# Holding the identity in the TensorE array across the sums of a decode attention kernel

## Chip, cores, metric

The kernel runs on one core of a Trainium2 chip. The metric is the device time of one execution in microseconds (us), taken as the median of repeated runs; "span" is the length of one profiled execution.

TensorE is written PE, and its weight loads PEld, since the profile records them apart. DVE is VectorE, ACT is ScalarE, SP issues the large transfers. A "chunk" is 32768 tokens of one head. There are 64 chunks (32 heads, 2 for each), and each has a K and a V load of 8.39 MB.

## The reference

One decode step of gated attention and a small feed-forward block, cut to what matters:

```python
def _A_ref(x, k_cache, v_cache, wq, wo):          # H, Sk, Dh = 32, 65536, 128
    q = ((x @ wq).reshape(B, Sq, H, Dh)).transpose(0, 2, 1, 3)
    scores = jnp.einsum("bhqd,bhkd->bhqk", q, k_cache) * (Dh ** -0.5)
    p = _softmax(scores, axis=-1)
    o = jnp.einsum("bhqk,bhkd->bhqd", p, v_cache)
    return o.transpose(0, 2, 1, 3).reshape(B, Sq, H * Dh) @ wo
# a = _A_ref(...); b = swiglu(x); return g * a + (1 - g) * b
```

The two caches are 1.07 GB in bf16 and are read once. Everything else is small.

## The kernel before

Tokens lie on partitions, so a score is a sum over the free axis. DVE multiplies K by q in place. PE then does most of the sum: with the identity as weights, sixteen matmuls of 512 columns accumulate sixteen slices of 8 head elements into 512 columns of a PSUM tile, and DVE reduces the last factor of 8.

```python
def group(key, parts, reads, writes):
    def fn():
        for out_ap, pairs in parts:
            for i, (a, b) in enumerate(pairs):
                ins = nc.tensor.matmul(              # a weight load and a matmul
                    out_ap, lhsT=a, rhs=b, start=(i == 0), stop=(i == len(pairs) - 1)
                )
        return ins
    op("PE", key, fn, reads, writes)

def block(n, j, m):                                  # m = 128 of a chunk's 256 columns of tokens
    dve("products", lambda: nc.vector.tensor_tensor(out=w, in0=w, in1=q_rep, op=ALU.mult), ...)
    B = 512 // R                                     # R = 8
    group(("sums", s, j, m, r),
          [(S_ps[r][:, b : b + B, :],
            [(ident, w[:, b : b + B, i * R : (i + 1) * R]) for i in range(Dh // R)])
           for b in range(0, m, B)],
          names + ["ident"], [("S_ps", r)])
# ... cut: gather (the last factor of 8, on DVE), exponential on ACT
# pv(n): 64 matmuls, weights are 4 columns of probabilities, 512 columns of V move
```

A chunk has two blocks of 32 sums and one value product of 64 matmuls. Three SBUF slots of 8.39 MB turn: while one is worked on, loads for the other two are issued. PE's instructions for the middle heads are a loop; the other engines' are written out.

```python
for n in range(N - 1):
    if n:
        load("k", n, [KPP])      # each waits until the last reader of its slot is done
        load("v", n, [KPP])
    for j in range(0, KPP, m):
        block(n, j, m)
        # ... cut: gather, exponential
    pv(n)
```

The softmax here doesn't subtract the row's maximum and nothing guards it: scores larger than these inputs give would overflow.

## Time and profile before

| | before |
|---|---|
| time, median of 3 | 2522.19 us |
| span of the profiled run | 2518.0 us |
| DMA rate, 100 to 2400 us | 434 GB/s |
| weight loads | 9115, of which 4096 of the identity for sums |

The first fence holds lines of the profile page: busy time, share of the span and number of instructions of each engine; busy tenths in 40 equal slices (9 is 90% or more), with the granted PE clock and the DMA rate; DMA queues with packets, MB and share of the 16 engines' span; the chain that ended last, by engine.

```profile
PE 1975.5 (78%) x9115; PEld 821.6 (33%) x9115; DVE 1268.3 (50%) x290; ACT 98.0 (4%) x402; POOL 1.9 (0%) x9
...
PE   4787877877778778778787787787877877878788
PEld 2233332333323333333333333333333332333334
...
DMA  9999999999999999999999999999999999999998
GB/s 423 431 432 432 434 434 437 433 433 433 433 436 434 435 433 436 434 433 433 434 435 436 433 433 433 434 434 434 435 434 436 433 433 433 433 435 436 435 433 369
...
q1 hardware_dynamic: 20880, 1087.78, 99.8%
q8 instruction: 16, 0.26, 0.0%
...
DMA 46%; PE 39%; DVE 13%; ACT 1%; another core or an unknown queue 0%; issue 0%; SPq 0%; DVEq 0%
```

DMA is full from the first slice to the last but one (9 tenths or more in each, the main queue at 99.8%). PE looks busy as well, at 78%, and the chain gives it 39%. Neither makes PE the limit. 78% leaves 22% of the span free (overlapping records are counted once in it: 704 sums of S_ps_102 of 382 ns each, 269 us, are 157.7 us on the page). And the chain runs through an instruction that frees a slot even if the load it lets go then waits behind other loads: at 1013.70 us it passes from 13.99 us of a value product to a K load of 34.86 us. The list of issues shows that queue (operation and count; the last column is the median us from issue to landing):

```profile
slot_67<-in_A_v_cache_dram SPq DMA_DIRECT2D x21, 32.7
...
slot_67<-in_A_k_cache_dram SPq DMA_DIRECT2D x21, 36.0
```

A load needs 19.3 us at 434 GB/s (8.39 MB over the rate), so by this estimate 13 to 17 us of older transfer are still ahead of it when it is issued.

The timeline of one chunk (start in us, length in us, engine, line, operation, output and inputs, count, then in brackets the idle time before it and what ended it):

```profile
1057.33 8.69 PE L265 MATMUL S_ps_101<-slot_67,ident 128*128 128x512 bf16 x32 [6.79 <-DVE slot_67 L324]
...
1066.99 7.08 PE L265 MATMUL S_ps_102<-slot_67,ident 128*128 128x512 bf16 x32
```

```profile
1057.73 0.15 PEld L265 LDWEIGHTS S_ps_101<-slot_67,ident 128*128 128x128 bf16 x1 [0.28 <-issue]
...
1066.98 6.59 PEld L265 LDWEIGHTS S_ps_102<-slot_67,ident 128*128 128x128 bf16 x32
```

The first block of a chunk comes after idle time and begins at half clock: the trace's clock records grant 0.5 of full speed from 1053.8 to 1060.6 us, and in the same view its weight loads start at 1057.73, 1058.16 and 1058.58, some 0.43 us apart. The second block runs at full clock (1.00 granted from 1066.98 to 1074.06); such matmuls are called warm here.

The last line concerns the end of the kernel, where the last value products run:

```profile
2511.11 1.74 PE L251 MATMUL m_c<-P_sb_84,slot_65 128*128 128x1 bf16 x60 [1.23 <-issue]
```

"issue" is idle time for which the profile finds no wait.

### The profile page before, as it was taken

How to read it: one execution, taken by the hardware profiler on the slowest of the kernel's cores; microseconds unless marked ns; L12 is line 12 of the kernel's file. 1: busy time of each engine (PE TensorE's matmuls, PEld its weight loads, DVE VectorE, ACT ScalarE, POOL GpSimd, SP SyncE). 2: the span in 40 equal slices, each digit the busy share in tenths (PEclk: the TensorE clock that was granted, in tenths of full speed). 3: DMA queues.
4: the chain of work that ended last, by engine and by line, in shares of the span. 5: the costliest groups of instructions: out<-in, count | busy, mean ns of one | idle time of the engine just before them, and what ended most of it. 6: DMA issues, size and time to landing. Idle time of an engine off the chain costs nothing.

```text
span 2518.0 us, 19423 instructions
## 1 busy us (share of the span) xinstructions
PE 1975.5 (78%) x9115; PEld 821.6 (33%) x9115; DVE 1268.3 (50%) x290; ACT 98.0 (4%) x402; POOL 1.9 (0%) x9
## 2 busy tenths in 40 slices
PE   4787877877778778778787787787877877878788
PEld 2233332333323333333333333333333332333334
DVE  3455364464553554645535546445455464464554
ACT  0000000000000000000000000000000000000000
POOL 0000000000000000000000000000000000000000
PEclk8888989989889889898898899898988989989898
DMA  9999999999999999999999999999999999999998
GB/s 423 431 432 432 434 434 437 433 433 433 433 436 434 435 433 436 434 433 433 434 435 436 433 433 433 434 434 434 435 434 436 433 433 433 433 435 436 435 433 369
DMA packets 20906, 1088.09 MB, mean 432 GB/s; under 512 B 2450, under 2 KB 2580, under 8 KB 2836
## 3 DMA queue, kind: packets, MB, share of 16 engines
q1 hardware_dynamic: 20880, 1087.78, 99.8%
q8 instruction: 16, 0.26, 0.0%
q14 instruction: 6, 0.05, 0.0%
q10 hardware_dynamic: 4, 0.00, 0.0%
HBM read 1087.77 MB, written 0.00 MB: 432 GB/s over the span
## 4 chain that ended last, share of the span: by engine, by line
DMA 46%; PE 39%; DVE 13%; ACT 1%; another core or an unknown queue 0%; issue 0%; SPq 0%; DVEq 0%
PE O_ps L251 18%; DMA slot_67<-in_A_k_cache_dram 16%; DMA slot_66<-in_A_k_cache_dram 15%; DMA slot_65<-in_A_k_cache_dram 14%; PE S_ps_101 L265 11%; PE S_ps_102 L265 9%; DVE slot_67 L324 4%; DVE slot_66 L324 4%; DVE slot_65 L324 3%; DVE S_sb_82 L349 2%; PE m_c L251 1%; DMA slot_65<-in_A_v_cache_dram 1%; ACT P_sb_83 L274 1%; PE m_x L265 0%
## 5 line engine op out<-in xcount | busy, mean ns | idle before, releaser
L265 PE MATMUL S_ps_101<-slot_65,ident 128*128 128x512 bf16 x672 | 196.5, 465 | 133.8 <-DVE slot_65 L324 133.8
L265 PE MATMUL S_ps_101<-slot_66,ident 128*128 128x512 bf16 x672 | 193.5, 459 | 133.5 <-DVE slot_66 L324 133.5
L265 PE MATMUL S_ps_101<-slot_67,ident 128*128 128x512 bf16 x704 | 195.2, 446 | 125.0 <-DVE slot_67 L324 125.0
L324 DVE TENSOR_TENSOR slot_67<-slot_67,q_bc_79 128x16384 bf16<-128x16384 bf16 (+1 forms) x28 | 208.2, 7469 | 144.0 <-DMA slot_67<-in_A_k_cache_dram 144.0
L349 DVE TENSOR_REDUCE S_sb_82<-S_ps_102 128x128 f32<-128x1024 f32 (+1 forms) x67 | 78.8, 1176 | 391.5 <-PE S_ps_102 L265 391.5
L324 DVE TENSOR_TENSOR slot_65<-slot_65,q_bc_78 128x16384 bf16<-128x16384 bf16 x22 | 190.2, 8688 | 148.1 <-DMA slot_65<-in_A_k_cache_dram 148.1
L324 DVE TENSOR_TENSOR slot_66<-slot_66,q_bc_78 128x16384 bf16<-128x16384 bf16 (+1 forms) x24 | 190.6, 7977 | 136.5 <-DMA slot_66<-in_A_k_cache_dram 120.9
L324 DVE TENSOR_TENSOR slot_66<-slot_66,q_bc_79 128x16384 bf16<-128x16384 bf16 x20 | 172.9, 8688 | 123.9 <-DMA slot_66<-in_A_k_cache_dram 123.9
L324 DVE TENSOR_TENSOR slot_65<-slot_65,q_bc_79 128x16384 bf16<-128x16384 bf16 x20 | 172.9, 8688 | 118.5 <-DMA slot_65<-in_A_k_cache_dram 118.5
L324 DVE TENSOR_TENSOR slot_67<-slot_67,q_bc_78 128x16384 bf16<-128x16384 bf16 x20 | 172.9, 8688 | 117.5 <-DMA slot_67<-in_A_k_cache_dram 117.5
L251 PE MATMUL O_ps<-slot_67,P_sb_83 128*4 128x512 bf16 x704 | 156.4, 383 | 28.8 <-ACT P_sb_83 L274 18.3
L251 PE MATMUL O_ps<-slot_65,P_sb_83 128*4 128x512 bf16 x704 | 153.7, 379 | 19.6 <-ACT P_sb_83 L274 19.6
L251 PE MATMUL O_ps<-slot_66,P_sb_84 128*4 128x512 bf16 x704 | 153.7, 379 | 19.3 <-ACT P_sb_84 L274 19.3
L265 PE MATMUL S_ps_102<-slot_67,ident 128*128 128x512 bf16 x704 | 157.7, 382 | 3.1 <-DVE slot_67 L324 3.0
L265 PEld LDWEIGHTS S_ps_101<-slot_65,ident 128*128 128x128 bf16 x672 | 75.9, 116 | 254.6 <-DVE slot_65 L324 144.4
L265 PEld LDWEIGHTS S_ps_101<-slot_66,ident 128*128 128x128 bf16 x672 | 75.0, 115 | 252.0 <-DVE slot_66 L324 144.3
L265 PEld LDWEIGHTS S_ps_101<-slot_67,ident 128*128 128x128 bf16 x704 | 76.8, 112 | 243.1 <-DVE slot_67 L324 136.1
L251 PE MATMUL O_ps<-slot_67,P_sb_84 128*4 128x512 bf16 x640 | 139.7, 379 | 18.3 <-ACT P_sb_84 L274 18.3
L251 PE MATMUL O_ps<-slot_65,P_sb_84 128*4 128x512 bf16 x640 | 139.7, 379 | 18.3 <-ACT P_sb_84 L274 18.3
L251 PE MATMUL O_ps<-slot_66,P_sb_83 128*4 128x512 bf16 x640 | 139.7, 379 | 17.5 <-ACT P_sb_83 L274 17.5
L265 PE MATMUL S_ps_102<-slot_66,ident 128*128 128x512 bf16 x672 | 148.8, 379 | 2.1 <-DVE slot_66 L324 2.1
L265 PE MATMUL S_ps_102<-slot_65,ident 128*128 128x512 bf16 x672 | 148.6, 379 | 0.2 <-DVE slot_65 L324 0.2
(83 smaller groups left out, 860.6 us busy)
## 6 DMA issues: line engine op xcount, KB each, us to landing
slot_66<-in_A_k_cache_dram SPq DMA_DIRECT2D x4, 2048.0 KB, 24.6
slot_67<-in_A_k_cache_dram SPq DMA_DIRECT2D x4, 2048.0 KB, 30.6
slot_65<-in_A_wq_dram SPq DMA_DIRECT2D x1, 4096.0 KB, 12.2
slot_66<-in_A_wo_dram SPq DMA_DIRECT2D x1, 4096.0 KB, 31.3
slot_65<-in_A_v_cache_dram SPq DMA_DIRECT2D x1, 4096.0 KB, 23.2
slot_65<-in_A_v_cache_dram SPq DMA_DIRECT2D x1, 2048.0 KB, 27.7
slot_65<-in_B_w_gate_dram SPq DMA_DIRECT2D x1, 1792.0 KB, 34.9
slot_65<-in_B_w_up_dram SPq DMA_DIRECT2D x1, 1792.0 KB, 38.6
```

Of the source, the lines that this page charges most:

```text
L251: ins = nc.tensor.matmul(out_ap, lhsT=a, rhs=b, start=start and i == 0, stop=stop and i == len(pairs) - 1,)
L265: ins = nc.tensor.matmul(out_ap, lhsT=a, rhs=b, start=(i == 0), stop=(i == len(pairs) - 1))
L274: "ACT", key, lambda: nc.scalar.activation(out=out_ap, in_=in_ap, func=func, **kw),
L324: "products", lambda: nc.vector.tensor_tensor(out=w, in0=w, in1=q_rep, op=ALU.mult),
L349: lambda: nc.vector.tensor_reduce(out=S_sb[b][:, :m], in_=S_ps[r][:, :m, :], axis=AXIS.X, op=ALU.add),
```

## The change

The identity is to be loaded into the array once for each block; the other 31 matmuls use the weights that the array holds. The intent is to spare 3962 of the 4096 identity loads.

```diff
         def fn():
+            held = None
             for out_ap, pairs in parts:
                 for i, (a, b) in enumerate(pairs):
-                    ins = nc.tensor.matmul(
-                        out_ap, lhsT=a, rhs=b, start=(i == 0), stop=(i == len(pairs) - 1)
-                    )
+                    first, last = i == 0, i == len(pairs) - 1
+                    if a is held:
+                        ins = nc.tensor.add_instruction(
+                            mybir.InstMatmult(
+                                name=nc.get_next_instruction_name(), engine=mybir.EngineType.PE,
+                                ins=[nc.tensor.lower_ap(b), weights],
+                                outs=[nc.tensor.lower_ap(out_ap)],
+                                start_tensor_calc=first, stop_tensor_calc=last,
+                                tile_size=(P, P), tile_position=(0, 0), ldweights=False,
+                            )
+                        )
+                    else:
+                        ins = nc.tensor.matmul(out_ap, lhsT=a, rhs=b, start=first, stop=last)
+                        weights = ins.ins.ins[1]
+                    held = a
             return ins
```

## The prediction

> **What bounds the kernel now.** DMA. The slice table has the DMA row at 9 in all slices but the last; the queue table gives the main queue 99.8% of the 16 engines' span. The stretch table gives 434 GB/s in every stretch of 400 to 500 us between 100 and 2400 us; 1087.78 MB at that rate is 2506 us of a span of 2518. [...]
>
> The chain of waits reads DMA 46%, PE 39%, DVE 13%. The 39% is no gain to be had: the chain walks from a load back to what freed its slot, but loads queue behind each other. A K load (8.39 MB) takes 19.3 us at 434 GB/s, and the issue list gives 36 us to landing (V: 32.5): some 17 and 13 us of older transfer are queued at issue. A slot freed earlier only lengthens that queue.
>
> Per 38.6 us of transfer (one K, one V load) PE needs, by the timeline, 8.4 to 10 and 7.07 us for two blocks of sums and 13.97 for the value product: about 30 us.
>
> **What changes.** In 134 blocks (4096 matmuls) the identity is loaded once each: 3962 weight loads of 98 to 116 ns go, about 425 us of PEld's 821.6. Nothing is added or moved; the other engines keep their order. But a load already overlaps the matmul before it: 32 warm matmuls take 7.07 us, 221 ns each; value products, with four-column weights, 218. [...] Cold matmuls at the head of first blocks start every 427 ns with 0.28 us between loads; they gain nothing. In all 8 to 17 us of PE time, which no DMA waits for.
>
> **Critical path.** Head: weights, K0 and V0 are queued within 5 us, before any sums. Middle: DMA bound. Tail: the last sums end before 2504.3 and their exponentials by 2505.4, while value pieces land up to about 2510; then unchanged products, a scale and the output DMA. The PE stall of 1.23 us at 2509.88, which the timeline calls "issue", may be instruction supply; with fewer PE instructions it may shift or vanish, worth up to about 1 us.
>
> **Prediction.** 2521.5 us, 8 in 10 between 2518.0 and 2525.0. Faster by over 2%: 0.01; within: 0.97; slower: 0.02.
>
> **What would show it.** Weight loads 9115 down to 5153; PEld busy near 395 us. Warm blocks of sums 6.9 to 7.05 us; first blocks still 8 to 10 us, 427 ns matmuls at their head. 434 GB/s unchanged; K issue to landing longer by at most 0.5 us. DVE's waits for K loads unchanged in total within 10 us.
>
> **What would make it wrong.** [...] both sum blocks at 427 ns are 27 us, with 14 for the value product 41 us against 38.6, and PE would become the limit. If each matmul without its own load waited for the pipe (379 ns, its shown duration), sums would take 24 us, 38 in all: just short of binding. [...] short stretches (404 to 448 GB/s) show no order by PE activity.

No trace or run shows: a ceiling for the DMA rate, of which the trace has only the measured 434 GB/s; the terms of the saving in PE time; and the mechanisms behind two dangers, that the array stays at half clock for want of weight loads, and that weight loads hinder DMA (the 27 and 41 us are for the first of the two). The saving came to 8 to 17 us of PE time in all. It was the author's estimate, 2 to 5 ns for each warm matmul, and the 6.9 to 7.05 us for a warm block follow from it. The forecast of 2521.5 us does not rest on these terms, since no DMA waits for that PE time.

## The result

| | before | after |
|---|---|---|
| median, same rounds | 2521.9 us (4 runs) | 2521.67 us (4 runs) |
| ratio, 95% interval | | 0.9997 (0.998 to 1.0014) |
| weight loads | 9115 | 5153 |
| PEld busy | 821.6 us | 410.4 us |
| PE busy | 1975.5 us | 1980.9 us |

Ratios are the mean time of one kernel's fast runs over that of the other's of the same rounds, so not quite the ratio of the medians quoted.

The page of the profile after, the same lines as before:

```profile
PE 1980.9 (79%) x9115; PEld 410.4 (16%) x5153; DVE 1268.7 (50%) x290; ACT 97.9 (4%) x402; POOL 1.9 (0%) x9
...
PEld 1111111111111111111111111111111111111113
...
DMA  9999999999999999999999999999999999999998
GB/s 423 431 432 433 434 435 435 433 435 437 433 434 433 434 433 435 436 436 433 434 435 435 433 434 433 434 434 437 434 436 433 434 437 433 434 433 433 433 431 361
...
q1 hardware_dynamic: 20880, 1087.78, 99.7%
q8 instruction: 13, 0.21, 0.0%
...
DMA 44%; PE 41%; DVE 13%; ACT 1%; issue 0%; another core or an unknown queue 0%; SPq 0%; DVEq 0%; ACTq 0%
```

Half of the weight load time is gone, and little else moved. The list of issues after shows the same queue ahead of each load:

```profile
slot_67<-in_A_v_cache_dram SPq DMA_DIRECT2D x21, 32.6
...
slot_67<-in_A_k_cache_dram SPq DMA_DIRECT2D x21, 36.0
```

The timeline of one chunk after, where a block now has one matmul with a load (L279) and 31 without (L269):

```profile
1017.42 0.61 PE L279 MATMUL S_ps_101<-slot_65,ident 128*128 128x512 bf16 x1 [4.88 <-DVE slot_65 L338]
1017.82 8.94 PE L269 MATMUL S_ps_101<-slot_65,ident 128*128 128x512 bf16 x31
...
1026.59 0.38 PE L279 MATMUL S_ps_102<-slot_65,ident 128*128 128x512 bf16 x1
1026.81 6.85 PE L269 MATMUL S_ps_102<-slot_65,ident 128*128 128x512 bf16 x31
```

The warm block runs from 1026.59 to 1026.81 + 6.85 = 1033.66: 7.07 us, as before. Start to start it is (6.85 - 0.379) / 30 = 216 ns. A count over all recorded sums gives the same median, 216 ns, before and after. So not even PE became faster. And the pause near the end is still there:

```profile
2512.66 2.01 PE L251 MATMUL m_c<-P_sb_84,slot_65 128*128 128x1 bf16 x70 [1.22 <-issue]
```

The time is unchanged, then. Two reasons are possible, and each alone would be enough. Either PE gained something that a full DMA hid (theory A), or PE gained nothing because the loads already ran behind the matmuls (theory B). The runs below separate them.

### The profile page after: what moved, and what is told of

It is laid out like the page before. It is cut to its first block, busy times and chain, and to the rows that moved or that the text cites. A ratio compares the mean times of both kernels' runs of the same rounds, so it can differ in the third digit from the quotient of the medians.

```text
span 2519.9 us, 15461 instructions
## 1 busy us (share of the span) xinstructions
PE 1980.9 (79%) x9115; PEld 410.4 (16%) x5153; DVE 1268.7 (50%) x290; ACT 97.9 (4%) x402; POOL 1.9 (0%) x9
## 2 busy tenths in 40 slices
DMA packets 20903, 1088.04 MB, mean 432 GB/s; under 512 B 2450, under 2 KB 2580, under 8 KB 2836
## 4 chain that ended last, share of the span: by engine, by line
DMA 44%; PE 41%; DVE 13%; ACT 1%; issue 0%; another core or an unknown queue 0%; SPq 0%; DVEq 0%; ACTq 0%
PE O_ps L251 18%; DMA slot_67<-in_A_k_cache_dram 16%; DMA slot_65<-in_A_k_cache_dram 14%; DMA slot_66<-in_A_k_cache_dram 14%; PE S_ps_101 L269 11%; PE S_ps_102 L269 9%; DVE slot_67 L338 4%; DVE slot_66 L338 4%; DVE slot_65 L338 3%; DVE S_sb_82 L363 2%; PE m_c L251 1%; PE S_ps_101 L279 1%; PE m_x L279 1%; ACT P_sb_83 L288 1%; DMA slot_65<-in_A_wq_dram 0%; PE S_ps_102 L279 0%
## 5 line engine op out<-in xcount | busy, mean ns | idle before, releaser
L269 PE MATMUL S_ps_101<-slot_67,ident 128*128 128x512 bf16 x680 | 191.3, 450 | 0.0
L269 PE MATMUL S_ps_101<-slot_65,ident 128*128 128x512 bf16 x651 | 187.1, 458 | 0.0
L269 PE MATMUL S_ps_101<-slot_66,ident 128*128 128x512 bf16 x650 | 185.3, 455 | 0.0
L269 PE MATMUL S_ps_102<-slot_67,ident 128*128 128x512 bf16 x680 | 152.4, 382 | 0.0
L269 PE MATMUL S_ps_102<-slot_65,ident 128*128 128x512 bf16 x651 | 143.9, 379 | 0.0
L269 PE MATMUL S_ps_102<-slot_66,ident 128*128 128x512 bf16 x650 | 143.9, 379 | 0.0
L279 PE MATMUL S_ps_101<-slot_65,ident 128*128 128x512 bf16 x21 | 12.8, 608 | 134.5 <-DVE slot_65 L338 134.5
L279 PE MATMUL S_ps_101<-slot_66,ident 128*128 128x512 bf16 x22 | 13.1, 597 | 130.5 <-DVE slot_66 L338 130.5
L279 PE MATMUL S_ps_101<-slot_67,ident 128*128 128x512 bf16 x24 | 13.9, 580 | 125.4 <-DVE slot_67 L338 125.4
## 6 DMA issues: line engine op xcount, KB each, us to landing
slot_66<-in_A_k_cache_dram SPq DMA_DIRECT2D x4, 2048.0 KB, 24.5
```

Of the source, the lines that this page charges most:

```text
L269: ins = nc.tensor.add_instruction(mybir.InstMatmult(name=nc.get_next_instruction_name(), engine=mybir.EngineType.PE, ins=[nc.tensor.lower_ ...
L279: ins = nc.tensor.matmul(out_ap, lhsT=a, rhs=b, start=first, stop=last)
```

## Experiments

In every experiment PE's loop is written out, so that all waits are on constants. The suffix "reload" means that the identity is loaded for each matmul, as before; "hold" means once for each block, as after.

### The loop written out: u_reload, u_hold

```diff
-        with nc.Fori(0, rounds, 1, engines=[PE], head_slot={PE: 0}) as r:
-            for i, o in enumerate(body[0]):
-                put(o, {s: val + r * step[i, s] for s, val in o.waits.items()})
+        for o in plan.ops:
+            if o.engine == "PE":
+                put(o, o.waits)
```

> The kernel before with the loop of the TensorE queue written out (all waits on constants), needed as a base for the other runs. Both theories (DMA bound; weight loads hidden) expect no effect: 2522 us within 0.3%, 434 GB/s, warm blocks of 32 sums still 7.07 us. If instruction supply for a straight stream of 18000 instructions mattered, it would be slower.

> The changed kernel with the loop written out. Both theories expect the same time as u_reload within 0.2%; weight loads 5153 instead of 9115. A rival, that fewer instructions ease supply once the stream is straight, expects it faster than u_reload by a measurable amount.

Measured: u_reload 2530.97 us (2530.22 to 2533.78), ratio to before 1.0037 (1.0023 to 1.0051); u_hold 2527.13 us (2526.71 to 2527.86), ratio 1.0022 (1.0009 to 1.0036). The kernel before took 2520.9 us in the same rounds. Both results were right.

The expectation of u_reload (2522 us within 0.3%) was missed: writing the loop out costs 10 and 6 us. The two runs lie within the 0.2% expected of u_hold, but their ranges do not overlap, so u_hold is some 4 us faster than u_reload, as the rival of its expectation had it. The queue lines of the two pages, u_reload first, then u_hold:

```profile
q1 hardware_dynamic: 20880, 1087.78, 99.3%
q8 instruction: 71, 1.16, 0.2%
```

```profile
q1 hardware_dynamic: 20880, 1087.78, 99.5%
q8 instruction: 56, 0.92, 0.1%
```

The instruction queue now fetches 71 and 56 packets of 16 KB, where the loop needed 16 and 13. This is a third thing that the change touches: it spares instructions, and instructions have to be fetched (3962 loads fewer, 15 packets fewer). With the loop, hardly anything is left to spare. The count of packets returns below.

### DMA taken off the path: light_reload, light_hold

```diff
         at = 0
+        if 2 <= n < N - 1:
+            pieces = [] if which == "v" else [HK]     # half of K, no V
         for m in pieces:
```

The result is wrong: stale data takes the place of what is not loaded. The runs passed the comparison with the reference all the same, so it proves nothing for them.

> Wrong result on purpose: from the third chunk on the V loads are left out and only half of each K chunk is loaded, so DMA needs about 9.7 us for each chunk instead of 38.6 and TensorE becomes the limit; the identity is loaded for every matmul. Expected about 30 us for each chunk (7.07 + 7.07 + 13.97 + the 1.75 us wait for the exponential), so about 2000 us in all, DMA share well under half.

> As light_reload with the identity held. Theory A (only DMA hid the gain; each matmul gains the 2 to 5 ns of the prediction) expects 8 to 20 us less than light_reload (0.4 to 1%). Theory B (the loads were already wholly behind the matmuls, start to start was 215.8 ns before the change) expects the same time within 0.2% although TensorE is now the limit.

Measured: light_reload 2009.49 us (2008.91 to 2011.48), light_hold 2009.65 us (2009.38 to 2011.75). The pages, light_reload first, then light_hold:

```profile
PE 1847.1 (92%) x9115; PEld 792.2 (39%) x9115; DVE 1263.4 (63%) x290; ACT 97.9 (5%) x402; POOL 1.9 (0%) x9
...
q1 hardware_dynamic: 12096, 320.22, 38.8%
...
PE 90%; DVE 6%; DMA 2%; ACT 1%; issue 0%; SPq 0%; DVEq 0%; ACTq 0%
```

```profile
PE 1844.9 (92%) x9115; PEld 410.0 (20%) x5153; DVE 1263.3 (63%) x290; ACT 97.8 (5%) x402; POOL 1.9 (0%) x9
...
q1 hardware_dynamic: 12096, 320.22, 38.8%
...
PE 90%; DVE 6%; DMA 3%; ACT 1%; issue 0%; SPq 0%; DVEq 0%
```

PE is the limit in both: the chain gives it 90%, and DMA is at 39%. Theory A wanted 8 to 20 us; the difference is 0.2 us the wrong way, inside the spread. Theory B holds: the loads cost PE no time.

### Shorter matmuls: c128 and c64

The thought behind these runs: if a load hides behind a matmul, a short enough matmul should uncover it. The sums are cut into pieces of 128 columns (four times as many matmuls) and of 64 (eight times).

```diff
-        B = 512 // R
+        B = 128 // R          # c64: 64 // R
```

> As light_reload (wrong result on purpose, TensorE the limit), with each sum of 512 columns cut into four matmuls of 128 columns, each with its own load of the identity. A warm matmul of 128 columns should take about a quarter of 215.8 ns, 54 ns, which no longer covers a load of 98 ns. [...] If loads never cost anything, about 2010 us.

> As c128_light_reload with the identity held for each block. Expected 54 to 56 ns for each matmul, blocks of about 7.2 us, 2010 to 2030 us in all: here the same edit should pay 15 to 25%. If holding the identity had a cost of its own for each matmul (a drain, a check), it would show here four times over.

The sentence cut from the first expectation put the time at 2400 to 2700 us if loads hide only behind long matmuls. Its upper end takes the recorded 98 ns for each load, 12.5 us for a block; its lower end, and with it the 15% of the second expectation, rested on a spacing that no run shows.

Measured: c128_light_reload 2040.64 us (2038.98 to 2043.5), c128_light_hold 2039.38 us (2039.01 to 2044.36). The expected gain of 15 to 25% is missing. c128_light_hold came out 9 us above its range of 2010 to 2030 us: four matmuls at 56 ns take 8 ns more than one at 216, which over 4096 of them makes an estimated 33 us, about what it took over light_hold (2009.65 us). The timeline of two blocks, reload first, then hold:

```profile
1012.87 14.47 PE L281 MATMUL S_ps<-slot,ident 128*128 128x128 bf16 x256
```

```profile
1012.78 0.23 PE L281 MATMUL S_ps<-slot,ident 128*128 128x128 bf16 x1
1012.85 7.25 PE L271 MATMUL S_ps<-slot,ident 128*128 128x128 bf16 x127
1019.94 0.22 PE L281 MATMUL S_ps<-slot,ident 128*128 128x128 bf16 x1
1020.00 7.25 PE L271 MATMUL S_ps<-slot,ident 128*128 128x128 bf16 x127
```

With a load for each, 256 matmuls take 14.47 us; with two loads in all, 1020.00 + 7.25 - 1012.78 = 14.47 us. The loads follow each other every 56 ns although each is recorded as 98 ns long. So the recorded length is not the time for which a load occupies PE. The step to 64 columns was meant to find that time.

> The missed expectation of the 128-column runs says that loads follow each other every 56 ns though each is recorded as 98 ns long, so the recorded length is not what a load occupies. Cut to 64 columns, each with its own load (wrong result on purpose, TensorE the limit): if a load occupies at most some 28 ns, a block stays near 7.2 us and the time near 2070 us; if it occupies between 28 and 56 ns, matmuls are spaced by it and a block of 256 takes 7.2 to 14.3 us, 2070 to 2900 us in all.

> The same with the identity held: 27 to 29 ns for each matmul of 64 columns, blocks of 7.0 to 7.5 us, 2040 to 2090 us. If this is clearly below c64_light_reload, the edit pays once matmuls are shorter than what a load occupies; if not, loads are hidden here too.

Measured: c64_light_reload 2325.56 us (2312.81 to 2333.64), c64_light_hold 2077.22 us (2076.98 to 2079.44). Here holding is worth 248 us. But it is not the loads that cost this. The timeline of two blocks (256 matmuls each) with reload:

```profile
1011.49 5.19 PEld L281 LDWEIGHTS S_ps<-slot,ident 128*128 128x128 bf16 x176 [0.44 <-issue]
...
1019.39 3.79 PEld L281 LDWEIGHTS S_ps<-slot,ident 128*128 128x128 bf16 x128 [2.70 <-issue]
1019.39 3.91 PE L281 MATMUL S_ps<-slot,ident 128*128 128x64 bf16 x128 [2.59 <-issue]
...
1025.33 7.63 PEld L281 LDWEIGHTS S_ps<-slot,ident 128*128 128x128 bf16 x208 [2.15 <-issue]
1025.33 7.75 PE L281 MATMUL S_ps<-slot,ident 128*128 128x64 bf16 x208 [2.04 <-issue]
```

and one block with the identity held:

```profile
1008.39 7.60 PE L271 MATMUL S_ps<-slot,ident 128*128 128x64 bf16 x255
```

While the stream with loads runs, 176 loads take 5.19 us, 29 ns each. That is the spacing of the held matmuls too. What is added are pauses, here of 2 to 3 us, with nothing to wait for. A count over the whole trace:

| | reload | hold |
|---|---|---|
| median start to start, 512 columns (light) | 216 ns | 216 ns |
| the same, 128 columns | 56 ns | 56 ns |
| the same, 64 columns | 29 ns | 29 ns |
| recorded length of an identity load | 98 ns | |
| pauses over 0.5 us without a wait, 64 columns | 92, together 166 us | none |
| matmuls started at half clock (53 to 54 ns), 64 columns | 2836 | 226 |

In the order of PE's recorded instructions, the distances between those pauses are 256, 768, 1024, 1280 and so on: 89 of the 91 are multiples of 256, and the other two miss one by 1. A fetched packet has 16 KB, and the packets counted give about as many instructions for each: the 32634 loads fewer of c64_light_hold spare 128 packets (167 against 295), 255 instructions a packet by this estimate. And every one of the 92 pauses ends 2.2 to 2.6 us after such a packet begins to be fetched, while at other matmuls of this run the last fetch began mostly 0.3 to 18 us earlier. The pauses are therefore PE waiting for its next packet of instructions. The time fits as well: 166 us of pauses, plus 2610 more matmuls at half clock of 24.5 ns each, 64 us, are 230 of the 248 us. The half clock comes with the pauses: without them, in the hold run, it is rare. Not every idle stretch brings it, though: in light_reload no matmul at half clock follows the 62 waits of 1.3 to 1.8 us for the exponential.

At full clock a load thus delays the matmuls by nothing that can be seen (216, 56 and 29 ns with and without it), and occupies PE for 29 ns at most. The rival in the expectation, a load of 28 to 56 ns that spaces the matmuls, falls.

The same explains the pause near the end of both main kernels. In the trace before, an instruction packet begins to be fetched at 2508.7 us and PE resumes at 2511.11; after, at 2510.3 and 2512.66. In both, 2.4 us lie between. In u_reload and u_hold, whose stream has no loop, no pause over 0.5 us without a wait is left.

### The full kernel with 128 columns: c128_reload, c128_hold

> The full kernel (all loads, right result) with sums of 128 columns, each with its own load. [...] So near the border: 2530 to 2800 us. Instruction bytes: some 2.7 MB instead of 1.16; if they cost 10 us for each MB, as the 9 us of u_reload for 0.9 MB suggest, 15 us more than u_reload even where TensorE does not bind.

> The full kernel with sums of 128 columns and the identity held. TensorE needs about 30 us of 38.6, so DMA still binds: u_hold plus the instruction bytes (0.79 MB more): 2527 us if they are free, about 2535 us if they cost 10 us for each MB. It should be faster than c128_reload.

The sentence cut from the first of these summed TensorE's work for a chunk to 37 to 43 us, against 38.6 of transfer; the lower end of that sum rested on the same spacing that no run shows.

Measured: c128_reload 2552.25 us (2551.28 to 2555.11), ratio 1.0126 (1.0109 to 1.0143); c128_hold 2538.81 us (2536.49 to 2541.38), ratio 1.0073 (1.0056 to 1.009). Both results were right.

c128_reload came out inside its wide range, c128_hold some 4 us above its higher figure. But TensorE does not bind in either, against what was thought possible for c128_reload: PE busy is 2006.3 and 2005.9 us, as good as equal. The difference of 13 us goes with the instructions again. The loads themselves are not its cause as far as the main pair shows: there 3962 of them went, and the time changed by 0.2 us. Over the kernel before of the same rounds, with the instruction packets of the profiled run:

| run | packets over the 16 of before | us over before | us for each packet |
|---|---|---|---|
| u_hold | 40 | 6.2 | 0.16 |
| u_reload | 55 | 10.1 | 0.18 |
| rep_two (below) | 47 | 10.4 | 0.22 |
| c128_hold | 88 | 17.8 | 0.20 |
| c128_reload | 151 | 31.3 | 0.21 |

In the light runs, where DMA is not the limit, 167 packets against 103 made no difference (2040.64 and 2039.38 us). So the time rises by about 0.2 us for each packet where DMA binds, and nothing where PE binds and is not starved. Bytes alone do not explain the size: 16 KB at 434 GB/s are 0.04 us. What makes up the rest was not shown and stays open.

### How much TensorE time is free: rep_two, rep_four_hold

The held kernel repeats the first half of each block of 32 sums, once in rep_two and twice in rep_four_hold (which then has 64 sums in a block, though it is not the whole block twice, as its expectation says). Each pass starts afresh, so the result stays right.

```diff
-                for b in range(0, m, B)
+                for b in ([0] * 1 if m == HK else []) + list(range(0, m, B))   # rep_four_hold: 2
```

> The changed kernel, written out, with one half of each block of sums done twice (right result): 16 matmuls more in each of two blocks, 6.9 us more TensorE work for each chunk, about 37 to 38.5 us of 38.6. DMA bound theory: at most a few us over u_hold (2527), say 2527 to 2537. If TensorE time were on the path, as the 39% of the chain of waits would have it, some 62 x 6.9 = 428 us more.

> The same with each block of sums done twice in full: 13.8 us more for each chunk, about 44 us of TensorE against 38.6 of transfer. TensorE must now be the limit: 62 x 44 plus head and tail, about 2780 to 2850 us, DMA below 90%. If it stayed near 2530, the slack would be larger than read.

Measured: rep_two 2532.14 us (2529.58 to 2533.76), ratio 1.0042 (1.0025 to 1.0059); rep_four_hold 2851.9 us (2851.28 to 2853.53), ratio 1.131 (1.1291 to 1.1329). The kernel before took 2521.72 us in the same rounds. The pages, rep_two first, then rep_four_hold:

```profile
PE 2284.5 (90%) x11067; PEld 409.6 (16%) x5153; DVE 1269.0 (50%) x290; ACT 97.9 (4%) x402; POOL 1.9 (0%) x9
...
q1 hardware_dynamic: 20880, 1087.78, 99.6%
...
PE 49%; DMA 37%; DVE 13%; ACT 1%; issue 0%; SPq 0%; DVEq 0%; ACTq 0%
```

```profile
PE 2686.1 (94%) x13019; PEld 409.8 (14%) x5153; DVE 1263.3 (44%) x290; ACT 97.8 (3%) x402; POOL 1.9 (0%) x9
...
q1 hardware_dynamic: 20880, 1087.78, 89.7%
...
PE 93%; DVE 4%; DMA 1%; ACT 1%; issue 0%; SPq 0%; DVEq 0%; ACTq 0%
```

In rep_two some 420 us of matmuls are added (1952 more, at 216 ns) and the time rises by 10 us, about what its 47 extra packets cost elsewhere. The chain reads PE 49% there, more than DMA's 37%, and PE time is still free. PE busy rises by only 304 us over the changed kernel, since a busier PE starts fewer sums at half clock: 106 sums follow the one before by 390 to 430 ns, against 644. Twice as much does not fit: in rep_four_hold DMA falls to 89.7%, PE sets the time, and it ends just above the stated range of 2780 to 2850 us. The slack for each chunk, counted in sums at 216 ns, thus lies between 6.9 and 13.8 us. An estimate from the times: rep_four_hold adds 3904 sums, 843 us, and takes 325 us more than u_hold, so 518 us fitted in, 8.5 us for each of the 61 chunks. The prediction's figures, 38.6 us of transfer against about 30 of PE work, put it at 8.6. The agreement is partly luck: some of the room came from the half clock, which all but vanishes there (27 such sums).

## Why the prediction was right

**DMA bounds the kernel.** Right, and shown. The rate is 434 GB/s before and after, the kernel absorbs 32 more sums, 6.9 us at 216 ns, in each chunk (rep_two), and it falls to 2009 us once most loads are left out (light_reload). Whether 434 GB/s is the most that DMA can move was not shown.

**The chain's 39% for PE is no gain to be had.** Right. The chain of rep_two gives PE 49% and 420 us more PE work still did not show.

**3962 weight loads go.** Right: 5153 remain. PEld busy was put near 395 us and is 410.4.

**A warm matmul gains 2 to 5 ns, 8 to 17 us of PE time in all.** Wrong: it gains nothing, and a warm block takes 7.07 us, not 6.9 to 7.05. The median start to start is 216 ns before and after, and with TensorE the limit the two versions take 2009.49 and 2009.65 us. The error was one of reading: 7.07 us over 32 counts the recorded tail of the last matmul. As DMA hid this term, the mistake did not reach the total.

**The pause of 1.23 us near the end may shift or vanish.** It shifted, to ten matmuls earlier in the stream, and kept its length, 1.22 us. That it is instruction supply is supported by the fetch that starts 2.4 us before it ends, as before the pauses of the 64-column run (2.2 to 2.6 us), and by its absence without the loop.

**K loads land up to 0.5 us later after issue; DVE's waits for them unchanged.** Right: 36.0 us in both, and 772.9 against 768.2 us of waits in total (the sum over the three slots).

**The listed dangers** did not come: the mean granted clock is 0.906 in both profiled runs, so missing loads did not slow the clock; a matmul without its own load did not wait for the pipe (216 ns, not 379); and the DMA rate stayed at 434 GB/s.

**What the prediction did not see** is that weight loads cost instruction fetches. With PE's loop no 16 KB packet of the instruction queue (q8) is fetched between 346 and 2468 us of the trace before, while the loop's body runs; there the change spares 3 packets, about 0.6 us at 0.2 us each (an estimate from the table above). That is too little to be seen in the interval of the main result.

## What to carry to other kernels

Do not count weight loads by their recorded length or their busy share: PEld fell from 39% to 20% at the same time with TensorE the limit (2009.49 and 2009.65 us). Compare start to start with and without them; here a load of 128 columns of bf16 weights was hidden behind every length of matmul tried, from 512 columns down to 64 (216, 56 and 29 ns, with loads and without). What a spared load did save here is an instruction, and that mattered when matmuls were so short that fetches starved PE (64 columns: 92 pauses, 166 us), or when straight code was fetched while DMA was already full (about 0.2 us for each packet of 16 KB, in five runs); the loop removed the second cost almost wholly (16 packets against 71 of u_reload, and 10 us). When a slot's load is issued while older transfers are still queued ahead of it for longer than a faster engine could save (here an estimated 13 to 17 us), work on that engine is off the path, whatever share the chain of waits gives it (here 39%, and 49% in rep_two, where 420 us more PE work came with 10 us more time).
